# A chain of attention, mixing MLP and gated experts: the expert stage taken apart into steps whose orders are written out in lists

## The chip, the cores and the metric

The kernel runs on one core of a Trainium2 chip. TensorE (PE) multiplies matrices, VectorE (DVE), ScalarE (ACT) and GpSimd (POOL) work on rows, and SyncE (SP) and POOL issue transfers. The metric is the device time of one launch in microseconds (us): the median of several runs.

## The reference

Three layers follow each other on 8 batches of 576 rows of 512 numbers.

```python
attn_out = softmax(q_chunk @ k_chunk.T / 8) @ v_chunk      # 8 heads of 64, chunks of 64 rows
x = sigmoid(xr @ w_r) * (relu(xk @ w_k) ** 2 @ w_v)        # xk, xr: x mixed with the row before
logits = x @ w_gate                                        # 4 experts, the best 2 of a row count
w = softmax over the 2 chosen logits
for e in range(4):                                         # causal attention of width 64
    a = softmax(causal(x @ wq[e] @ (x @ wk[e]).T / 8))
    out += (row chose e) * w * (a @ (x @ wv[e]) @ wo[e])
```

The output has 8 x 576 x 512 numbers in float32. `wq`, `wk` are drawn wide, so that scores are large.

## The kernel before

All matrix products are kept precise by splitting each factor into a high and a low part: `mm3` (L95 to L97) issues hi x hi, lo x hi, hi x lo for each product. Attention weights and V are split too, but with two parts side by side in one operand.

The first 616 us compute the first two layers, in an order written out in the lists `START` and `TWO_UNITS`. They leave the result as `x2T` in DRAM, hi and lo. The function `experts()` does the third layer from 616 us on, and the change lies in it alone.

`experts()` goes through the 8 batches (counted from 0). A batch has two pairs of experts (p) and each pair 9 steps: four query tiles of 128 rows for each of two experts, and the last 64 rows for both experts at once. So a batch has 18 steps (`SB`). A step runs through these functions:

- `t_S`: scores of one tile on PE (L753, `Sps`, as wide as the causal part, 128 to 576 columns), masked negated row maximum on DVE (L755, `sm`, `nm`), Exp on ACT (L765, `P`, with the row sum into `z`).
- `t_T`, three steps later: PE transposes `P` in blocks of 128 (L806, `Tps`), ACT copies the high part (L812, `PTh`), DVE takes the low part (L813, `PTl`).
- `t_AV`, when the tiles of a group (0 to 1, or 2 to 4) are through: PE multiplies with V (L835, L839, `AVps`), ACT copies one half (L849, `yt`), DVE adds the other (L850, `Yf`).
- `t_scale` when a pair is through: the row sums `z` with the gate's weight `gp` on DVE (L778 to L781), transposed on PE (L783), sent through DRAM by SP and spread over the partitions (`zb`). `t_Y`: POOL multiplies `Yf` by `zb` (L855), DVE rounds to `Yh` (L84, also `Y4h` for the last 64 rows), POOL takes the rest `Yl`, `Y4l` (L866).
- `t_out`: output projection (`pj<-woh,Yh`, L95 to L97), ACT copies `o` (L879), SP stores it.

Between the steps lies the preparation of the next pair or batch: `p_load` (POOL issues four loads of `x2`, L616, into the only buffer), `p_qk` (K and Q from `x2`, 12 matmuls of 288 columns for each half; ACT, DVE, copies by SP, and `Ql` on POOL, L649), `p_v` (V and the 4 gate logits in one product of 260 columns; ACT L697, DVE L698, L699), `p_v4` (the last 64 rows of two batches at once, from `x0` loaded at L673) and `p_gate` (L705 to L728: ranks and weights of the experts; seven operations until ACT's Exp L718, five behind it; four of the twelve run on POOL: L709, L711, L717, L723).

Which step issues which piece is fixed by numbers in `CFG`; but the order on each engine is made by the scheduler of the framework, which knows the dependences and a priority for each instruction. Two lines tell it about the filling work:

```python
with tc.issue_after(last.ins) if CFG["after"] else nullcontext():
    for f in fill.get(i, ()):
        f()
```

PSUM gives 2 banks to `Sps`, 3 to `Tps`, 1 to `AVps`, 2 to `pj`; there are 5 buffers of `P` and 3 of `sm`. Each engine takes its instructions strictly in order, so an instruction that waits holds up all behind it on that engine.

Of the kernel before, what the change touches and what calls it, by code (L numbers as in the profile page):

```python
# [59 lines left out]
FIRST_UNITS, FIRST_PAIRS = 2, 6  # L60
CFG = dict(ps=(2, 3, 1, 2), P=5, sm=3, load=5, lag=(3, 4), out=(5, 1), qk1=(1, 1), qk0=(9, 1.1), v=(10, 0.9), order=((3, 0), (2, 0), (0, 0), (4, 0), (1, 0), (3, 1), (2, 1), (0, 1), (1, 1)), after=1, conv='v', clo='v', chi='g', x2hi='g', x2lo='v', ylo='g', yhi='v', xt='aa', r2='av', klo='vv', amul='vv', nearly=2, x2b=1, yb=4, qb=4, direct=((0, 1), (1, 1), (1, 1)), tailAV=4, kp=2, yt=1, yf=2, zb=1, om=(3, 2, 1, 0, 4), hp=1000, x2d=2, early=(2, 1), dact=3, rate0=0.43, rate=0.45, sh=(10, 12, 2), sh2=(11, 1, -1), pro='cccqqaacavvcaaaaacaacaaaascc', alag=2, seq=0, end=2, outL=(11, 2), outE=2, kcp='aa', dsc='v', ldb=2, vb=2, cn=512, stb=2, xb=4, pa=5, tb=2, first_j=7, dve_j=6)
# [514 lines left out]
def experts(tc, at_pool, weights, out, x2T, w_gate, wq, wk, wv, wo, ident, dram, B, S):  # L576
# [3 lines left out]
    nc = tc.nc  # L580
# [11 lines left out]
    groups = [(0, 2), (2, NT)]  # L592

    with ExitStack() as ctx:
# [34 lines left out]
        def p_qk(b, p, nm, h):  # L629
            ws = w_q if nm == "Q" else w_k  # L630
            cc = slice(h * HB, (h + 1) * HB)
            pc = slice(p * 128, (p + 1) * 128)
            pp = ps.tile([128, DM], F32, tag="pj", bufs=CFG["ps"][3], name="pj")[:, :HB]
            x = x2[b]
            mm3(nc, pp, [((ws[g][0][:, pc], ws[g][1][:, pc]), (x.hi[:, g, cc], x.lo[:, g, cc])) for g in range(KD)])
            two = (b * EP + p) % 2
            if nm == "Q":
                if h == 0:
                    for i in range(2):
                        Q[b, 2 * p + i] = px.tile([128, S], F32R, tag="Q", bufs=CFG["qb"], name="Q")  # L640
# [10 lines left out]
            if h == 0:
                K[b, p] = [px.tile([128, S], F32R, tag="Kp" + x, bufs=CFG["kp"], name="Kp" + x) for x in "hl"]
            t, l = K[b, p]
            nc.scalar.activation(out=t[:, cc], in_=pp, func=ACTF.Copy)
            nc.vector.tensor_tensor(l[:, cc], pp, f32(t[:, cc]), op=ALU.subtract)
            if h == 1:
                for i in range(2):
                    KD2[b, 2 * p + i] = d = px.tile([128, SF], F32R, tag="K", bufs=CFG["qb"], name="K")
                    for j in range(2):
                        nc.sync.dma_start(out=f32(d[half[j]]), in_=f32(t[half[i], :SF]))  # L660
                    nc.sync.dma_start(out=f32(KL[two][i][half[i]]), in_=f32(l[half[i], :SF]))
# [6 lines left out]
        def p_v4(b):  # L668

            x = sb.tile([128, 2, KD, 2, 64], F32R, tag="x0", bufs=1, name="x0")  # L670
# [4 lines left out]
            xh, xl = (x[:, i].rearrange("p g j t -> p g (j t)") for i in range(2))  # L675
            pp = ps.tile([128, DM], F32, tag="pj", bufs=CFG["ps"][3], name="pj")[:, :NV]
            mm3(nc, pp, [((xh[:, g], xl[:, g]), (w_v[g][0][:, :NV], w_v[g][1][:, :NV])) for g in range(KD)])
            for j in range(2):
                V4[b + j] = v = V4s[(b + j) % 3]
                G[b + j] = g = sb.tile([128, NT, E], F32, tag="lg", bufs=3, name="lg")  # L680
                r = half[j]
                pv = pp[r, :E * D].rearrange("p (e d) -> p e d", e=E)
                nc.scalar.activation(out=v[:64, :, 0], in_=pv, func=ACTF.Copy)
                nc.vector.tensor_tensor(v[:64, :, 1], pv, f32(v[:64, :, 0]), op=ALU.subtract)
                nc.vector.tensor_copy(g[r, LT], pp[r, E * D:])
                nc.gpsimd.tensor_copy(v[64:, :, 0], f32(v[:64, :, 0]))
# [356 lines left out]
```

## Time and profile before

| | us |
|---|---|
| median of 3 runs | 981.07 (980.85 to 982.61) |
| the profiled run | 981.03 |
| its span, first to last instruction | 978.7 |
| PE busy in the span | 937.5 |
| DVE busy | 662.0 |
| ACT busy | 622.5 |
| POOL busy | 206.0 |
| the expert stage, in the span | 616 to 978.7 |

The profile comes from one execution. A timeline row is one instruction: start, duration, engine, source line, operation, output and inputs with their shapes; in brackets how long the engine stood before it and whose end it waited for. Matmuls overlap, so their rate is read from start to start. A table of stretches gives busy time and the granted clock of PE, 1.00 being full speed.

### The profile page before, as it was taken

What the parts mean: (1) busy time and instruction counts of PE and PEld (TensorE: products, weight loads), DVE (VectorE), ACT (ScalarE), POOL (GpSimd) and SP (SyncE); (2) the same over time, 40 slices, a digit from 0 to 9 for tenths busy, and PEclk for the clock granted to TensorE, in tenths of its full rate; (3) what the DMA queues carried; (4) which work ended last, traced back from release to release, by engine and by line L of the source; (5) the groups of instructions that cost most, each with busy time, mean ns of one, the idle gap of its engine ahead of it and who ended that gap; (6) DMA issues with size and microseconds to landing.
All of it is one profiled execution on the core that took longest, in us unless ns stands there. A gap on an engine that the chain in (4) does not pass through costs nothing.

```text
span 978.7 us, 21549 instructions
## 1 busy us (share of the span) xinstructions
PE 937.5 (96%) x8022; PEld 904.4 (92%) x8022; DVE 662.0 (68%) x1625; ACT 622.5 (64%) x1417; POOL 206.0 (21%) x392
## 2 busy tenths in 40 slices
PE   2689999999999999999999999999999999999997
PEld 2589999999999999999999999898989998999995
DVE  7999746657565755575566612677877787778795
ACT  3598466665756574757576732667675677667684
POOL 3111111101120202020202115513333333323111
PEclk9799999999999999999999999999999999999999
DMA  9884433444324543444322217656362845445322
GB/s 250 203 197 127 87 84 81 86 87 98 83 67 91 114 72 73 81 108 73 77 68 80 59 47 160 135 138 184 68 187 67 211 73 169 123 136 142 99 55 88
DMA packets 223408, 108.39 MB, mean 111 GB/s; under 512 B 187352, under 2 KB 199752, under 8 KB 223304
## 3 DMA queue, kind: packets, MB, share of 16 engines
q1 hardware_dynamic: 193032, 67.16, 30.1%
q0 software_dynamic: 30272, 39.86, 15.5%
q8 instruction: 64, 1.05, 0.5%
q14 instruction: 40, 0.33, 0.1%
HBM read 66.01 MB, written 28.38 MB: 96 GB/s over the span
## 4 chain that ended last, share of the span: by engine, by line
PE 89%; DVE 5%; DMA 4%; issue 1%; ACT 1%; SPq 0%; POOL 0%; POOLq 0%; ACTq 0%; DVEq 0%
PE mps L95 17%; PE mps L96 17%; PE mps L97 17%; PE pj L95 7%; PE pj L96 6%; PE pj L97 6%; PE Sps L753 5%; PE Tps L806 4%; PE AVps L839 2%; PE AVps L835 2%; PE Tps L187 2%; DMA x<-x2T 2%; PE PVps L267 1%; PE Sps L211 1%; DMA ldq<-in_q_dram 1%; DMA st<-in_moe_w_v_dram 1%
## 5 line engine op out<-in xcount | busy, mean ns | idle before, releaser
L95 PE MATMUL mps<-xhk,wkh 128*128 128x384 f32 x384 | 130.7, 340 | 0.0
L95 PE MATMUL mps<-kh,wvh 128*128 128x384 f32 x384 | 129.6, 339 | 0.0
L96 PE MATMUL mps<-xlk,wkh 128*128 128x384 f32 x384 | 129.0, 336 | 0.0
L97 PE MATMUL mps<-xhk,wkl 128*128 128x384 f32 x384 | 129.0, 336 | 0.0
L96 PE MATMUL mps<-kl,wvh 128*128 128x384 f32 x384 | 128.5, 335 | 0.0
L97 PE MATMUL mps<-kh,wvl 128*128 128x384 f32 x384 | 128.4, 334 | 0.0
L370 DVE TENSOR_TENSOR kl<-r,kh 128x384 fp32r<-128x384 f32 x96 | 53.8, 561 | 87.4 <-ACT kh L366 86.8
L765 ACT ACTIVATE P<-sm,nm 128x512 f32<-128x512 f32 (+3 forms) x144 | 83.9, 584 | 22.1 <-DVE nm L755 15.6
L755 DVE CUSTOM_DVE_ANT_0 sm<-Sps,mask 128x256 f32<-128x256 f32 (+4 forms) x160 | 74.5, 477 | 29.5 <-PE Sps L753 28.7
L84 POOL CAST x2d<-x2o 128x384 fp32r<-128x384 f32 x48 | 33.5, 702 | 271.9 <-DVE x2o L387 268.5
L813 DVE TENSOR_TENSOR PTl<-Tps,PTh 128x512 fp32r<-128x512 f32 (+2 forms) x144 | 70.2, 505 | 4.9 <-ACT PTh L812 2.9
L95 PEld LDWEIGHTS mps<-xhk,wkh 128*128 128x128 f32 x384 | 72.2, 188 | 0.6
L95 PEld LDWEIGHTS mps<-kh,wvh 128*128 128x128 f32 x384 | 72.0, 188 | 0.4
L96 PEld LDWEIGHTS mps<-xlk,wkh 128*128 128x128 f32 x384 | 72.2, 188 | 0.0
L97 PEld LDWEIGHTS mps<-xhk,wkl 128*128 128x128 f32 x384 | 72.2, 188 | 0.0
L96 PEld LDWEIGHTS mps<-kl,wvh 128*128 128x128 f32 x384 | 72.1, 188 | 0.0
L97 PEld LDWEIGHTS mps<-kh,wvl 128*128 128x128 f32 x384 | 72.1, 188 | 0.0
L308 DVE SCALAR_TENSOR_TENSOR xa<-XT,mu,xa 128x384 f32<-128x384 f32 x96 | 60.3, 637 | 15.9 <-ACT xa L304 15.7
L364 ACT ACTIVATE r<-mps 128x384 f32<-128x384 f32 x96 | 46.4, 484 | 37.3 <-PE mps L97 37.2
L304 ACT ACTIVATE xa<-XT,mu 128x384 f32<-128x384 f32 x96 | 57.5, 614 | 18.6 <-DVE xlr L319 17.3
L812 ACT ACTIVATE PTh<-Tps 128x512 fp32r<-128x512 f32 (+2 forms) x144 | 61.6, 453 | 8.5 <-PE Tps L806 7.1
L806 PE MATMUL Tps<-ident,P 128*128 128x128 f32 x384 | 63.9, 274 | 2.7 <-DVE z L768 1.4
(183 smaller groups left out, 2629.3 us busy)
## 6 DMA issues: line engine op xcount, KB each, us to landing
x2T<-x2d POOLq DMA_DIRECT2D x48, 384.0 KB, 3.1
x<-x2T POOLq DMA_DIRECT2D x32, 576.0 KB, 6.5
K<-Kph SPq DMA_DIRECT2D x64, 128.0 KB
out_dram<-o SPq DMA_DIRECT2D x32, 256.0 KB
ldk<-in_k_dram SPq DMA_DIRECT2D x192, 32.0 KB
ldq<-in_q_dram SPq DMA_DIRECT2D x192, 32.0 KB
ldv<-in_v_dram SPq DMA_DIRECT2D x21, 256.0 KB
st<-in_moe_w_k_dram SPq DMA_DIRECT2D x8, 512.0 KB
```

Source lines behind the costliest of these rows:

```text
L95: nc.tensor.matmul(out=out, lhsT=ah, rhs=bh, start=first and i == 0, stop=False)
L96: nc.tensor.matmul(out=out, lhsT=ah, rhs=bl, start=False, stop=False)
L97: nc.tensor.matmul(out=out, lhsT=al, rhs=bh, start=False, stop=last and i == n - 1)
L304: nc.scalar.activation(out=a, in_=XT[u][:, g, :, :SEG], func=ACTF.Copy, scale=mu1[:, w, g:g + 1])
L308: nc.vector.scalar_tensor_tensor(a, XT[u][:, g, :, 1:], mu[:, w, g:g + 1], a, op0=ALU.mult, op1=ALU.add)
L370: eng(nc, CFG["klo"][u >= CFG["nearly"]]).tensor_tensor(o.lo, K2.pop((u, m)), f32(o.hi), op=ALU.subtract)
L753: issued = nc.tensor.matmul(out=pp[:, :w], lhsT=x, rhs=y[:, a:a + w], start=n == 0, stop=n == len(terms) - 1)
L755: nc.vector.tensor_tensor_reduce(out=sm[:, a:a + w], in0=pp[:, :w], in1=mk[:, :w], op0=ALU.add, op1=ALU.min, scale=-scale, scalar=3e38, ac ...
L765: nc.scalar.activation(out=x[:, :nk], in_=sm[:, :nk], func=ACTF.Exp, scale=-1.0, bias=nm[:, :1], accum_out=z)
L806: nc.tensor.transpose(pp[:, j], x[:, j * 128:(j + 1) * 128], ident)
L812: nc.scalar.activation(out=h, in_=src, func=ACTF.Copy)
L813: nc.vector.tensor_tensor(l, src, f32(h), op=ALU.subtract)
```

## The change

The functions of the stage are cut at every change of engine. `p_qk` becomes q, qh, ql, kd, qp; `p_v` and `p_v4` become v, vh, vl, vp and lx; `p_gate` gr, ge, gw, gp; `t_S` S, X, E, C; `t_scale` z, zt, zr, zd; `t_T` T, H, L; `t_AV` A, I, F; `t_Y` M, N, O; `t_out` o, oe, od; `p_load` ld. The first 18 steps, batch 0, are scheduled as before. From batch 1 on the pieces are recorded in the order of a list, `TWO_BATCHES` for batches 1 and 2 and again for 3 and 4, `LAST_BATCHES` for 5, 6 and 7, and each instruction is tied to the one recorded before it on its engine, POOL's and SP's transfers included. The four gate operations that ran on POOL run on DVE.

```diff
+FREE_STEPS = 18
+TWO_BATCHES = """
+z-1,1 T-1,15 q0,1,0 S0,2 X0,2 H-1,15 q0,1,1 qh0,1,1 zt-1,1 zr-1,1 L-1,15 E0,2 T-1,17 S0,1 X0,1 S0,0 X0,0 qh0,1,0
...
+""".split()
+LAST_BATCHES = """
+S0,1 T-1,16 z-1,1 X0,1 T-1,17 S0,0 H-1,16 L-1,16 T-1,15 S0,2 X0,0 zt-1,1 X0,2 q0,1,0 E0,1 zr-1,1 zd-1,1 S0,3 H-1,17
...
+""".split()
...
-            nc.gpsimd.tensor_tensor(c1, c1, before.unsqueeze(1).to_broadcast(sh), op=ALU.mult)
+            nc.vector.tensor_tensor(c1, c1, before.unsqueeze(1).to_broadcast(sh), op=ALU.mult)
             nc.vector.tensor_tensor(c2, lj, li, op=ALU.is_gt)
-            nc.gpsimd.tensor_tensor(c1, c1, c2, op=ALU.add)
+            nc.vector.tensor_tensor(c1, c1, c2, op=ALU.add)
...
-            nc.gpsimd.tensor_tensor(x, l, m.unsqueeze(2).to_broadcast([128, NT, E]), op=ALU.subtract)
+            nc.vector.tensor_tensor(x, l, m.unsqueeze(2).to_broadcast([128, NT, E]), op=ALU.subtract)
...
-            nc.gpsimd.tensor_tensor(l, x, m.unsqueeze(2).to_broadcast([128, NT, E]), op=ALU.mult)
+            nc.vector.tensor_tensor(G[b], x, m.unsqueeze(2).to_broadcast([128, NT, E]), op=ALU.mult)
...
-            at(n + L1, lambda b=b, p=p, t=t, i=i: t_T(b, p, t, i))
+            k = divmod(n, SB)
+            at(n + L1, ("T", *k), ("H", *k), ("L", *k))
...
-                last = t_S(*steps[i])
-            with tc.issue_after(last.ins) if CFG["after"] else nullcontext():
-                for f in fill.get(i, ()):
-                    f()
-            for f in todo.get(i, ()):
-                f()
+                first = [("S", *k), ("X", *k), ("E", *k)] + ([("C", *k)] if steps[i][:2] in direct else [])
+            if i >= FREE_STEPS:
+                rest += first + fill.get(i, []) + todo.get(i, [])
+                continue
+            last = run(first[:1]) or last
+            run(first[1:])
+            with tc.issue_after(last.ins):
+                run(fill.get(i, []))
+            run(todo.get(i, []))
...
+        order = [f for b in range(1, B - 3, 2) for f in named(TWO_BATCHES, b)] + list(named(LAST_BATCHES, B - 3))
+        assert sorted(order) == sorted(rest)
+        traced, prior = nc.cur_bb.bb.instructions, {}
+        for f in order:
+            at0 = len(traced)
+            run([f])
+            for ins in traced[at0:]:
+                if ins.engine in prior:
+                    tc.add_manual_dep(ins, prior[ins.engine].name,
+                                      mybir.DependencyInfo(mybir.DependencyClass.NoSync, mybir.DependencyReason.DATA),
+                                      reason="order of the last steps")
+                prior[ins.engine] = ins
```

A name such as `T-1,15` is step 15 of the batch before the list's first. A dependence of class NoSync sets an order and adds no wait of its own.

On POOL, at the load of batch 3's inputs (`x2T_66`; L616 of the kernel before at 717.20 us), the order before is this; `gp` is the gate's weights, `Yf<-Yf,zb` the scaling, `Yl` and `Y4l` the split behind it, `Ql` a copy for the last 64 rows.

```order
L728 COPY gp<-lg 64x2 x2
L616 DMA x_9513<-x2T_66 128x2x576 x4
L855 TENSOR_TENSOR Yf<-Yf,zb 128x576
L649 CAST Ql_7594<-Q 64x64 x4
L866 TENSOR_TENSOR Yl<-Yf,Yh 128x512
L866 TENSOR_TENSOR Y4l<-Yf,Y4h 128x64
L855 TENSOR_TENSOR Yf<-Yf,zb 128x576
L866 TENSOR_TENSOR Yl<-Yf,Yh 128x512
L866 TENSOR_TENSOR Y4l<-Yf,Y4h 128x64
```

The changed kernel has this at the same load (L683 there).

```order
L1013 TENSOR_TENSOR Yf<-Yf,zb 128x576
L1031 TENSOR_TENSOR Yl<-Yf,Yh 128x512
L1031 TENSOR_TENSOR Y4l<-Yf,Y4h 128x64
L1013 TENSOR_TENSOR Yf<-Yf,zb 128x576
L1031 TENSOR_TENSOR Yl<-Yf,Yh 128x512
L1031 TENSOR_TENSOR Y4l<-Yf,Y4h 128x64
L739 CAST Ql_7594<-Q 64x64 x4
L683 DMA x_9625<-x2T_66 128x2x576 x4
L835 COPY gp<-lg 128x2x8
```

The scaling and the split stood behind the load and the copies; now two of each stand ahead of the load, and the gate's weights behind it.

On ACT, where batch 5 begins, the order before is as follows; `V` is the copy of the value projection, `gx` the gate's Exp, `P` the attention's Exp, `Kph` and `Q` copies of projections.

```order
L697 ACTIVATE V_11118<-pj_11266 128x4x64
L849 ACTIVATE yt_11569<-AVps_11564 64x256
L765 ACTIVATE P_11429,z_11430<-sm_11423,nm_11424 128x512
L654 ACTIVATE Kph_11459<-pj_11446 128x288
L765 ACTIVATE P_11444,z_11430<-sm_11438,nm_11439 128x384
L765 ACTIVATE P_11486,z_11430<-sm_11480,nm_11481 128x128
L718 ACTIVATE gx_11314<-gx_11314 128x20
L654 ACTIVATE Kph_11459<-pj_11488 128x288
L812 ACTIVATE PTh2_7973<-Tps_11579 128x4x128
```

The changed kernel has this there; `PTh0` are copies of transposes, and the last V copy is that of `pj_11339`.

```order
L783 ACTIVATE V_11187<-pj_11318 128x4x64
L783 ACTIVATE V_11187<-pj_11339 128x4x64
L998 ACTIVATE yt_11379<-AVps_11372 64x256
L896 ACTIVATE P_11386,z_11044<-sm_11381,nm_11382 128x128
L822 ACTIVATE gx_11400<-gx_11400 128x20
L896 ACTIVATE P_11421,z_11044<-sm_11354,nm_11355 128x256
L965 ACTIVATE PTh0_7971<-Tps_11426 128x128
L896 ACTIVATE P_11470,z_11471<-sm_11431,nm_11432 128x384
L965 ACTIVATE PTh0_7971<-Tps_11434 128x2x128
```

Five instructions stood between the last V copy and the gate's Exp; now two do, and the P of 256 columns (`P_11421`) stands right behind the gate's Exp.

On PE the changed kernel has, from the last matmul of that value projection on:

```order
L159 MATMUL pj_11339<-wv_7341,x2_11050 128x260
L868 MATMUL Sps_11360<-K_10948,Q_10912 128x128
L868 MATMUL Sps_11360<-Kl11_7592,Q_10912 128x128
L990 MATMUL AVps_11372<-PTh0_7971,V_10427 128x256
L986 MATMUL AVps_11372<-PTl0_7972,V_10427 64x128
L986 MATMUL AVps_11372<-PTl0_7972,V_10427 64x256
L990 MATMUL AVps_11372<-PTh0_7971,V_10427 128x256
L868 MATMUL Sps_11423<-K_11402,Q_11283 128x384
L868 MATMUL Sps_11423<-Kl00_7589,Q_11283 128x384
L945 MATMUL Tps_11426<-ident_60,P_11386 128x128
L945 MATMUL Tps_11434<-ident_60,P_11421 128x128 x2
L868 MATMUL Sps_11437<-K_11402,Q_11283 128x512
L868 MATMUL Sps_11437<-Kl00_7589,Q_11283 128x512
```

The transposes of `P_11421` come eight matmuls and one transpose behind the value projection. In the kernel before, an AV group, four score matmuls of 512 and 384 columns and the 12 matmuls of a K projection follow the value projection.

## Rows read from the trace of the kernel before

**Rows 1.** Head of the page and busy time of PE.

```profile
span 978.7 us, 21549 instructions
...
PE 937.5 (96%) x8022; PEld 904.4 (92%) x8022; DVE 662.0 (68%) x1625; ACT 622.5 (64%) x1417; POOL 206.0 (21%) x392
```

**Rows 2.** Stretches: PE, PEld, DVE, ACT, POOL busy (count), granted clock, DMA share, GB/s.

```profile
715.00:728.00 13.00, 12.46 (x86) 11.01 (x85) 12.01 (x42) 11.17 (x34) 6.81 (x11) 1.00 0.78 221
728.00:804.00 76.00, 76.00 (x567) 72.97 (x566) 54.96 (x184) 49.79 (x141) 21.81 (x47) 1.00 0.51 120
804.00:817.00 13.00, 12.45 (x87) 11.05 (x85) 12.01 (x42) 11.16 (x34) 6.80 (x11) 1.00 0.81 225
...
960.00:966.00 6.00, 5.80 (x28) 4.59 (x29) 3.93 (x13) 2.03 (x7) 2.98 (x3) 0.72 0.00 0
```

**Rows 3.** Timeline of PE: start, duration, engine, line, operation, idle before it.

```profile
718.69 0.28 PE L753 MATMUL Sps<-Kl,Q 128*128 128x256 f32 x1
719.08 0.65 PE L839 MATMUL AVps<-PTh,V 128*128 128x320 f32 x3
...
723.44 0.41 PE L806 MATMUL Tps<-ident,P 128*128 128x128 f32 x2 [0.40 <-DVE PTl L813]
723.89 0.50 PE L95 MATMUL pj<-woh,Yh 128*128 128x512 f32 x1
```

**Rows 4.** Timeline of DVE in the same place.

```profile
723.42 0.42 DVE L84 CAST Yh<-Yf 128x512 fp32r<-128x512 f32 x1
```

**Rows 5.** Timeline of POOL in the same place.

```profile
717.20 2.93 POOL L616 DMA_DIRECT2D x<-x2T  x4 [5.62 <-PE pj L97]
720.19 1.42 POOL L855 TENSOR_TENSOR Yf<-Yf,zb 128x576 f32<-128x576 f32 x1
```

**Rows 6.** Timeline of PE: two waits near the end.

```profile
943.27 0.49 PE L753 MATMUL Sps<-K,Q 128*128 128x512 f32 x1 [0.42 <-DVE nm L755]
...
960.13 0.44 PE L806 MATMUL Tps<-ident,P 128*128 128x128 f32 x2 [1.02 <-DVE z L768]
```

**Rows 7.** Timeline of PE: starts without a wait.

```profile
703.56 0.34 PE L753 MATMUL Sps<-K,Q 128*128 128x384 f32 x1
...
703.91 0.28 PE L95 MATMUL pj<-wv,x 128*128 128x260 f32 x1
704.03 0.28 PE L96 MATMUL pj<-wv,x 128*128 128x260 f32 x1
```

**Rows 8.** ACT by line and shape, 640 to 979: busy, mean ns, idle before.

```profile
L765 ACT ACTIVATE P<-sm,nm 128x256 f32<-128x256 f32 x30 | 15.2, 508 | 2.6 <-DVE nm L755 2.1
...
L697 ACT ACTIVATE V<-pj 128x256 fp32r<-128x256 f32 x28 | 10.8, 384 | 13.9 <-PE pj L97 13.8
...
L718 ACT ACTIVATE gx<-gx 128x20 f32<-128x20 f32 x7 | 1.5, 212 | 0.4 <-POOL gx L717 0.3
```

**Rows 9.** DVE by line and shape, 640 to 950, same columns.

```profile
L698 DVE TENSOR_TENSOR V<-pj,V 128x256 fp32r<-128x256 f32 x28 | 11.7, 419 | 3.4 <-ACT V L697 3.0
...
L708 DVE TENSOR_TENSOR c<-lg 128x80 f32<-128x80 f32 x7 | 1.7, 237 | 0.1
```

**Rows 10.** An input load: first issue on POOL, its late reader; below, another load's landing.

```profile
672.25 2.92 POOL L616 DMA_DIRECT2D x<-x2T  x4
...
684.54 0.40 PE L95 MATMUL pj<-x,wk 128*128 128x288 f32 x1 [0.92 <-DMA x<-x2T]
...
x<-x2T POOLq DMA_DIRECT2D x4, 576.0 KB, 5.8
```

**Rows 11.** DVE beside POOL: a slow row, POOL's, and that line's mean.

```profile
667.99 1.07 DVE L759 TENSOR_TENSOR nm<-nm 128x1 f32<-128x1 f32 x1
...
667.63 1.42 POOL L855 TENSOR_TENSOR Yf<-Yf,zb 128x576 f32<-128x576 f32 x1 [1.73 <-issue]
...
L759 DVE TENSOR_TENSOR nm<-nm 128x1 f32<-128x1 f32 x15 | 3.1, 205 | 0.0
```

More of the change, by code (lines that the diff above doesn't have):

```diff
@@ L592, in experts @@
     groups = [(0, 2), (2, NT)]
+    cols = [slice(tiles[a][0], tiles[z - 1][0] + tiles[z - 1][1]) for a, z in groups + [(0, NT)]]
+    SB = EP * len(CFG["order"])
+    steps = [(b, p, t, i) for b in range(B) for p in range(EP) for t, i in CFG["order"]]
+    n = len(CFG["order"])
+    steps[-n:] = [(B - 1, EP - 1, t, i) for g in (1, 0) for t, i in CFG["order"] if groups[g][0] <= t < groups[g][1]]
     with ExitStack() as ctx:
@@ L651, in p_qk @@
[L651 to L661, printed above, removed]
+            mm3(nc, proj((b, p, n), HB), [((ws[g][0][:, pc], ws[g][1][:, pc]), (x.hi[:, g, cc], x.lo[:, g, cc]))
+                                          for g in range(KD)])
@@ new lines, in qk_hi @@
+        def qk_hi(b, p, n):
+            pp, h = PJ[b, p, n], n % 2
+            cc = slice(h * HB, (h + 1) * HB)
+            if n // 2:
+                for i in range(2):
+                    if (b, 2 * p + i) not in Q:
+                        Q[b, 2 * p + i] = px.tile([128, S], F32R, tag="Q", bufs=CFG["qb"], name="Q")
+                for i in range(2):
+                    nc.scalar.activation(out=Q[b, 2 * p + i][half[i], cc], in_=pp[half[i]], func=ACTF.Copy)
+                return
+            if (b, p) not in K:
+                K[b, p] = [px.tile([128, S], F32R, tag="Kp" + x, bufs=CFG["kp"], name="Kp" + x) for x in "hl"]
+            nc.scalar.activation(out=K[b, p][0][:, cc], in_=pp, func=ACTF.Copy)
@@ L664, in experts, with k_copies @@
+        def k_copies(b, p):
+            two, (t, l) = (b * EP + p) % 2, K[b, p]
+            for i in range(2):
+                KD2[b, 2 * p + i] = d = px.tile([128, SF], F32R, tag="K", bufs=CFG["qb"], name="K")
+                for j in range(2):
+                    nc.sync.dma_start(out=f32(d[half[j]]), in_=f32(t[half[i], :SF]))
+                nc.sync.dma_start(out=f32(KL[two][i][half[i]]), in_=f32(l[half[i], :SF]))
         V4s = [sb.tile([128, E, 2, D], F32R, bufs=1, name=f"V4{i}") for i in range(3)]
@@ L702, in p_gate, with v_pool, g_rank @@
+        def v_pool(b):
+            for j in range(2):
+                v, g = V4[b + j], G[b + j]
+                nc.gpsimd.tensor_copy(v[64:, :, 0], f32(v[:64, :, 0]))
+                nc.gpsimd.tensor_copy(g[half[1 - j], LT], g[half[j], LT])
+        def g_rank(b):
             l = G[b]
@@ L911, in experts @@
             nc.gpsimd.memset(before[:, i, 0:i], 1.0)
-        p_gate(0)
+        run([(f, 0) for f in GATE])
         for p in range(EP):
@@ L928, in experts, with at @@
         nc.vector.memset(f32(PTs[0][0][:, :, 1, :128]), 0.0)
[L929 to L934 removed]
         todo, fill = {}, {}
[L937 to L938 removed]
+        def at(i, *fs):
+            todo.setdefault(int(i), []).extend(fs)
         def spread(base, nm, fs):
```

377 lines of the change are left out of this document (249 added, 128 removed).

## The prediction, made before the changed kernel ran

> **What bounds the kernel now.** I read the page's head first, then a table of busy time by stretch, then the matmul timeline at the few stretches that are not full, and there the engine that was waited for. The head gives a span of 978.7 us with PE busy for 937.5 us, 96% [rows 1]; the profiled run took 981.03 us, so 2.3 us lie outside the span, and it stands 0.04 us under the median of 981.07. The sum below is made against the span, and 2.3 us are added at its end. The change touches nothing ahead of the expert stage (from 616 us on). In that stage the long stretches are full: 728 to 804 us shows PE busy for 76.00 of 76.00 us, all at the full clock, while DVE has 54.96 us of work and ACT 49.79 [rows 2]. No order can gain anything there, since the matmuls are the same in both kernels. [...]
>
> **The waits that go.** (1) At 719 to 724 us PE stands three times. Matmuls start 0.12 us apart with 260 columns (703.91 to 704.03) [rows 7] and, as an estimate, half that with 128. Counted from start to start against this, PE is late by 0.27 us at 719.08 (0.39 behind a matmul of 256 columns at 718.69), by about 0.6 at 723.44 (the page's own figure for the idle part is 0.40, since it takes matmuls by their ends), and by 0.23 at 723.89 behind two transposes [rows 3], together 1.1 us. The last of them waits for Yh, the rounding of the attention rows that the output projection reads; DVE has it only at 723.42 [rows 4]. Yh needs the scaled rows from POOL, and POOL does the scaling only at 720.19 because the load of the next batch's inputs stands ahead of it in the queue, issued at 717.20 after POOL had waited 5.62 us for the last matmul that reads the old inputs [rows 5]. The changed order on POOL puts the scaling and the split in front of that load, so the scaling no longer waits for those matmuls. I take all of the 1.1 us: three times, 3.4 us with rounding. From below it is the 0.23 us of the Yh wait alone, 0.7 in all, because the other two pieces wait for DVE and could come back in another order. (2) At 943.27 us PE waits 0.42 us for a row maximum on DVE [rows 6]; with the late starts around it I count 0.7 us, and the new order puts other matmuls between. From below 0. (3) In the tail PE waits 1.02 us for DVE at 960.13 [rows 6], and there are some 4 us more in smaller pieces and at the halved clock. Laying out the new list of the last batch by the same pitches I still find about 3.8 us in waits, against 5.1 now. I take 1.0 us; from above 2.7 if the clock doesn't fall (it ran at half for 3.4 us, worth 1.7), from below -1.7 if it falls twice.
>
> **The waits that come.** (4) Where the second pair of batches ends and the list of the last three begins, the new orders have little matmul work behind the last value projection. PE has two score matmuls of 128 columns, one AV group, the scores of 384 columns and one transpose, and then two transposes of the 256-column P; but on ACT that P's Exp stands behind the gate's Exp, which needs the whole gate, which needs the logits of that last projection. The chain from the last projection matmul's start: 0.28 until its result [rows 7], V's copy 0.384 [rows 8], its difference 0.419, then the logits' copy and seven gate operations, eight small ones at 0.237 each at most [rows 9] and at 0.15 each if their starts overlap (an estimate), 1.2 to 1.9, gate Exp 0.212 and P 0.508 [rows 8]: 3.0 to 3.7 us. PE's work meanwhile: 0.12 for the last projection matmul [rows 7], 0.12 for the two score matmuls of 128 columns, 0.42 for the AV group (three matmuls of 256 columns and one of 128), 0.35 for the scores of 384 columns (703.56 to 703.91) [rows 7] and 0.1 for a transpose, 1.1 us. So PE waits 1.9 to 2.6 us. Behind it the next bank of scores must be freed by the row maximum of the 384 columns, which DVE has behind five gate and three z operations, and this adds 0.1 to 0.6. I take 2.6 us of 2.0 to 3.2, once. Zero would hold only if PE were itself late by so much at that place, which the full stretches speak against. (5) At the beginnings of batches 1 and 3 the transpose of z stands behind 3.4 and 4.3 us of matmul work, and its z on DVE stands behind the whole gate: the same chain to the gate's Exp (about 3.0), and then five gate operations and three of z at 0.2 each (1.6), 4.6 us. That is 1.2 and 0.3 us at most, and nothing where DVE overlaps its starts: 0.5 each, 1.0 in all. (6) The load of x2 has one buffer, so from the last matmul on the old inputs to the first on the new ones PE must live on other work. Before, the orders put 67 to 117 matmuls there, 11.1 to 17.5 us by their pitches; one load is late nevertheless, issued from 672.25 on and waited for at 684.54 for 0.92 us [rows 10], 12.3 us behind the first issue. After, there are 54 to 70 matmuls, 9.5 to 11.9 us. The load issued at 717.20 would need 2.93 us for the four issues [rows 5] and 5.8 us to land [rows 10], 8.7 us, so a load takes 8.7 to 12.3. I take 0.5 us at each of three tight loads, less the one that goes (1.0): +0.4; bounds -1.0 (no load is late) and +4.6 (two of the three tight ones take 12.3: 2 x 2.8 less 1.0).
>
> **What costs nothing.** The four gate operations that move from POOL to DVE add 4 x 0.237 = 0.95 us of DVE per batch [rows 9], in full stretches beside 54.96 of 76.00 us busy [rows 2]; elsewhere than at (4) and (5) the row maxima and differences around them have that room. If not, 7 x 0.95 = 6.6 us. Fewer interruptions of matmul groups change nothing that the pitch rows show. SP's queue gets a fixed order too, with the same K copies and stores; the scale's copies have at least 6.7 us of matmuls before the output projection that needs them.
>
> **The sum.** -3.4 -0.7 -1.0 +2.6 +1.0 +0.4 = -1.1 us: span 977.6, time 979.9 us.
>
> **Rivals.** A, the gains come without the new waits: DVE and ACT catch up in the slack between small instructions, so (4), (5) and (6) fall away and the 684.54 wait goes as well: -3.4 -0.7 -1.0 -1.0 = -6.1, time 974.9 us. For it: DVE and ACT are idle in a quarter to a third of a full stretch [rows 2]. Against it: the order on each engine is binding, so idle time elsewhere doesn't shorten the chain at (4). B, slower: the gate on DVE is held up by POOL. The row minimum at 667.99 took 1.07 us where its line has a mean of 0.205, and it ended as POOL's scaling did (667.63, 1.42 us long) [rows 11]. Before, the gate's multiplications ran on POOL itself, one after the other with the scaling; now seven operations in a row on DVE read two inputs each while POOL may scale (1.42) or split (1.30). With two such hits of 0.87 us at each of the three ends of a list, where the chain has no slack, 5.2 us come on top: -1.1 + 5.2 = +4.1, time 985.1 us. It decides as soon as the gate's chain there is over about 4 us. Against it: the order on POOL has the scaling mostly well before or behind the gate.
>
> [...]
>
> That the list does not do what it says, with the chip running as before, would give 981 us; the bound matmul work makes a result near that likely anyway, and I count it within the forecast.
>
> **How the numbers follow.** About 0.2%, 2 us, is what a measurement here can tell from no change: faster is under 979.1, slower over 983.0. The forecast has 0.45, with its own range of 977 to 983; of it 0.13 lies under 979.1 and 0.30 between, 0.02 over. Rival A has 0.30, nearly all faster (0.28 and 0.02). Rival B has 0.25, of it 0.23 slower and 0.02 between. Together faster 0.41, same 0.34, slower 0.25. The range runs from A's time less 1.4 us (half of the tail's upper bound), 973.5, to just over B's, 985.7.
>
> **What would show it.** Right: in the changed kernel's matmul timeline the output projection behind each input load has no wait for Yh, and POOL shows the scaling ahead of the load; near the start of the sixth batch one wait of 2 to 3 us of the two transposes for ACT's P, with the gate's Exp in front of it. Wrong: that wait is under 1 us (toward A), or row maxima and gate operations take over 0.8 us beside POOL at the ends of lists (toward B); a wait of over 1.5 us for an x2 load would break the term (6); and a tail with more than one stretch at half clock the term (3).

## The result, and the profile after

The changed kernel takes 993.0 us (median of 6 runs, 989.9 to 994.3) against 981.2 us (6 runs, 980.3 to 982.6) for the kernel before: the ratio is 1.0119, with a 95% interval of 1.0107 to 1.0131. It is slower by 11.8 us, where 979.9 us had been forecast, and outside the range. The profiled run took 993.39 us. The page's head, to be read against [rows 1]:

```profile
span 991.6 us, 21443 instructions
...
PE 942.6 (95%) x8022; PEld 907.0 (91%) x8022; DVE 665.4 (67%) x1657; ACT 623.0 (63%) x1417; POOL 195.8 (20%) x360
```

The span is 12.9 us longer with the same 8022 matmuls. Since the matmuls of the expert stage are the same and nearly in the same order of kinds, the two traces can be laid beside each other by matmul work done: at which time has PE got through the same amount? The table is worked out so from all matmul starts, each matmul counted with the usual distance to the next start for its shape; each row is one such amount.

| before, us | after, us | behind, us | what lay in between |
|---|---|---|---|
| 616.2 | 616.5 | 0.3 | |
| 664.5 | 666.0 | 1.5 | batch 0, scheduled in both |
| 688.8 | 691.2 | 2.4 | the first list begins; load of batch 2 |
| 719.6 | 721.7 | 2.1 | |
| 727.5 | 728.9 | 1.4 | the place where PE waited for Yh |
| 736.5 | 742.2 | 5.7 | load of batch 3 |
| 767.8 | 774.9 | 7.1 | the list begins again; load of batch 4 |
| 809.7 | 816.4 | 6.7 | |
| 822.6 | 831.6 | 9.0 | Yh again; load of batch 5 |
| 837.6 | 846.6 | 9.0 | |
| 844.7 | 856.8 | 12.1 | the list of the last three begins |
| 973.8 | 986.9 | 13.1 | batches 5 to 7 and the tail |

So the loss comes in three steps of 4.3, 2.3 and 3.1 us, 9.7 of the 12.8 us between the first row and the last, and some small ones. The 1.4 us between 736.5 and 767.8 us are the largest of these; PE has no wait over 0.25 us there, and they were not traced. The waits of PE from 616 us on, by line and by what was waited for (us in total, times, longest), name the first two:

```profile
PE pj L157 <- DMA x<-x2T: 8.0, 8, 2.5
PE Tps L945 <- ACT P L896: 2.9, 4, 1.5
PE Tps L945 <- DVE P L906: 2.1, 3, 1.4
```

Before, PE waited 1.7 us in all for x2 loads; now 8.0 us. The busy table of stretches (columns as in [rows 2]) shows it around batch 3's load, and below that at the third step:

```profile
724.00:733.00 9.00, 9.00 (x52) 7.78 (x51) 6.05 (x25) 6.00 (x16) 2.85 (x4) 1.00 0.93 279
733.00:736.40 3.40, 0.93 (x8) 0.70 (x6) 0.84 (x4) 0.74 (x3) 0.00 (x0) 1.00 0.77 264
736.40:741.00 4.60, 4.60 (x25) 4.60 (x26) 1.32 (x7) 1.74 (x6) 0.51 (x3) 0.63 0.01 3
...
845.00:853.00 8.00, 5.68 (x42) 4.79 (x42) 7.20 (x33) 3.98 (x15) 2.97 (x9) 1.00 0.29 62
853.00:905.00 52.00, 52.00 (x390) 49.81 (x389) 39.09 (x132) 36.80 (x103) 14.83 (x26) 1.00 0.53 130
```

From 724 to 733 us PE is full. From 733.0 to 736.4 it is busy for 0.93 of 3.40 us while all other engines are nearly idle too and DMA is at 0.77. Then it runs for 4.6 us at a granted clock of 0.63, which means 0.37 x 4.6 = 1.7 us lost on top: from 738 to 740 us the granted clock was 0.50. Behind 853 us PE is full again, at the full clock (52.00 of 52.00, 1.00).

**Why the load is late.** The timeline of POOL there (start, duration, operation, idle before it), to be read against [rows 5]:

```profile
717.55 1.44 POOL L1013 TENSOR_TENSOR Yf<-Yf,zb 128x576 f32<-128x576 f32 x1 [2.49 <-DMA zb<-sc]
...
722.91 0.82 POOL L739 CAST Ql<-Q 64x64 fp32r<-64x64 f32 x3 [0.75 <-DVE Q L730]
723.93 2.92 POOL L683 DMA_DIRECT2D x<-x2T  x4 [0.20 <-PE pj L159]
```

The timeline of PE, to be read against [rows 3], from the last matmul on the old inputs to the late one on the new:

```profile
720.34 0.30 PE L159 MATMUL pj<-x,wq 128*128 128x288 f32 x1
...
722.28 0.48 PE L157 MATMUL pj<-woh,Yh 128*128 128x512 f32 x1
...
732.51 0.30 PE L157 MATMUL pj<-x,wk 128*128 128x288 f32 x1
...
736.35 0.40 PE L157 MATMUL pj<-x,wk 128*128 128x288 f32 x1 [2.47 <-DMA x<-x2T]
```

The timeline of DVE, the first row to be read against [rows 4]:

```profile
719.02 0.43 DVE L146 CAST Yh<-Yf 128x512 fp32r<-128x512 f32 x1 [0.19 <-POOL Yf L1013]
...
722.33 0.94 DVE L730 TENSOR_TENSOR Q<-pj,Q 64x288 fp32r<-64x288 f32 x2 [1.03 <-ACT Q L718]
```

The scaling now stands ahead of the load and runs at 717.55, Yh is ready by 719.45, and the output projection at 722.28 has no wait for it. That part of the change works. But between the scaling and the load stand four Ql copies on POOL, and the last three of them wait for DVE's part of Q, which comes at 722.33 since DVE itself waited 1.03 us for ACT's part. The last matmul that reads the old inputs ended at 720.64; the load is issued at 723.93, 3.3 us later. In the kernel before, it was 0.5 us (716.70 to 717.20 [rows 5]). The load's last quarter then lands at 736.30, 12.4 us after the first issue, where before it took 9.4 us (717.20 to 726.64). The DMA engines in these 12.4 us:

```profile
GB/s 0 0 0 0 37 88 44 81 125 162 258 376 435 383 410 409 413 412 420 398 413 413 420 413 383 394 395 353 363 371 365 387 351 394 364 402 205 34 26 20
...
q0 software_dynamic: 1088, 2.36, 63.9%
q1 hardware_dynamic: 569, 1.04, 23.7%
...
out_dram<-o SPq DMA_DIRECT2D x4, 256.0 KB
```

They move 351 to 435 GB/s for most of the time: 2.36 MB of the load, and 1.04 MB more on the other queue, which are the four output stores that SP issued from 725.03 to 734. In the kernel before, SP issued no store between 717 and 727 us. As an estimate from the row, the stores' 1.04 MB take 2.6 us at some 400 GB/s, of the 3.0 us by which this load took longer.

**The third step** is the wait that the prediction had put at the start of batch 5. The timeline of PE there:

```profile
848.12 0.34 PE L868 MATMUL Sps<-Kl,Q 128*128 128x384 f32 x1
848.97 0.33 PE L945 MATMUL Tps<-ident,P 128*128 128x128 f32 x1 [0.50 <-ACT P L896]
850.77 0.44 PE L945 MATMUL Tps<-ident,P 128*128 128x128 f32 x2 [1.47 <-ACT P L896]
...
852.36 0.33 PE L868 MATMUL Sps<-K,Q 128*128 128x128 f32 x1 [0.35 <-DVE nm L878]
```

The timeline of ACT, the gate's Exp and the P behind it:

```profile
850.00 0.22 ACT L822 ACTIVATE gx<-gx 128x20 f32<-128x20 f32 x1 [1.09 <-DVE gx L817]
850.13 0.49 ACT L896 ACTIVATE P<-sm,nm 128x256 f32<-128x256 f32 x1
```

The timeline of DVE, the row maximum behind the gate and z:

```profile
851.74 0.55 DVE L878 CUSTOM_DVE_ANT_0 sm<-Sps,mask 128x384 f32<-128x384 f32 x1
```

PE waits 0.50 us for one P, 1.47 us for the next, whose Exp starts at 850.13 right behind the gate's Exp at 850.00, and 0.35 us for a bank that the row maximum at 851.74 must free. Counted from start to start the first two are 0.7 and 1.7 us, and the table gives 3.1 us in all.

### The profile page after: what moved, and what is told of

It is laid out like the page before. It is cut to its first block, busy times and chain, and to the rows that moved or that the text cites. A ratio compares the mean times of both kernels' runs of the same rounds, so it can differ in the third digit from the quotient of the medians.

```text
span 991.6 us, 21443 instructions
## 1 busy us (share of the span) xinstructions
PE 942.6 (95%) x8022; PEld 907.0 (91%) x8022; DVE 665.4 (67%) x1657; ACT 623.0 (63%) x1417; POOL 195.8 (20%) x360
## 3 DMA queue, kind: packets, MB, share of 16 engines
q8 instruction: 63, 1.03, 0.4%
## 4 chain that ended last, share of the span: by engine, by line
PE 81%; DMA 8%; DVE 7%; POOL 1%; issue 1%; SPq 1%; ACT 1%; POOLq 0%; DVEq 0%; ACTq 0%
PE mps L157 17%; PE mps L158 17%; PE mps L159 17%; PE pj L157 6%; PE pj L159 5%; PE pj L158 5%; DMA x<-x2T 4%; PE Sps L868 3%; PE Tps L945 3%; PE AVps L990 2%; PE Tps L249 2%; PE AVps L986 2%; PE PVps L329 1%; PE Sps L273 1%; DMA ldq<-in_q_dram 1%
## 5 line engine op out<-in xcount | busy, mean ns | idle before, releaser
L896 ACT ACTIVATE P<-sm,nm 128x384 f32<-128x384 f32 (+4 forms) x144 | 83.5, 581 | 14.0 <-DVE nm L878 11.6
L965 ACT ACTIVATE PTh<-Tps 128x128 fp32r<-128x128 f32 (+4 forms) x160 | 65.2, 434 | 23.9 <-PE Tps L945 22.4
L969 DVE TENSOR_TENSOR PTl<-Tps,PTh 128x512 fp32r<-128x512 f32 (+3 forms) x144 | 71.3, 507 | 7.9 <-ACT PTh L965 6.6
```

Source lines behind the costliest of these rows:

```text
L896: nc.scalar.activation(out=x[:, :sm.shape[1]], in_=sm, func=ACTF.Exp, scale=-1.0, bias=nm, accum_out=z_column(at)[0])
L965: nc.scalar.activation(out=h, in_=src, func=ACTF.Copy)
L969: nc.vector.tensor_tensor(l, src, f32(h), op=ALU.subtract)
```

## The experiments

In all lists the names are those of the change: ld is the load of x2, lx that of the last rows, od an output store, gr to gp the gate, E an Exp, qp the Ql copies, zd the copies of the scale, zt the transpose of z. "PE's stage time" below is from the first score matmul to the last matmul of the profiled run: 357.6 us before, 370.5 us after. Ratios are to the kernel before on the same chip; the changed kernel's is 1.0119 (1.0107 to 1.0131), and gains and losses against it are differences of these ratios. The runs are numbered as their names are; there is no fifth.

**1. The load ahead of the Ql copies** (batches 3 and 5)

```diff
-... qp1,1 S1,12 H1,4 L1,4 A1,0,0 E1,10 T1,10 ld2 I1,0,0 ...
+... N0,1,2 O0,1,2 ld2 qh1,1,2 ... qp1,1 S1,12 H1,4 L1,4 A1,0,0 E1,10 T1,10 I1,0,0 ...
```

> The list of two batches is changed in one place: the load of the second batch's inputs (batches 3 and 5) stands ahead of the four Ql copies on POOL instead of behind them. Theory (the load is issued late: 3.3 us after the last matmul that reads the old inputs, because the Ql copies ahead of it wait for DVE's part of Q): the load is issued about 2.8 us earlier at both places, PE's wait for it falls from 2.5 and 2.7 us to under 0.6 each, and the time falls by 4 to 5.5 us, from 993.0 to about 988. Rival (the load is slow because output stores share the DMA engines, so that it ends when the stores end): it lands no more than 1 us earlier, and the time stays at 991 to 993.

Measured: 987.6 us (986.3 to 989.1), ratio 1.0076 (1.0061 to 1.0091), 0.43% or 4.2 us less than the changed kernel; PE's stage time is 363.0 us. POOL's timeline in this run:

```profile
719.80 2.91 POOL L683 DMA_DIRECT2D x<-x2T  x4
722.70 1.14 POOL L739 CAST Ql<-Q 64x64 fp32r<-64x64 f32 x4
```

PE's timeline, the first matmul on the new inputs:

```profile
731.37 0.30 PE L157 MATMUL pj<-x,wk 128*128 128x288 f32 x1
```

The load is issued at 719.80, 0.3 us behind the last reader, and the Ql copies follow it. The first matmul on the new inputs at 731.37 has no wait and neither have those behind it, though the stores still run beside the load. The late issue was enough to make the wait.

**2. Three stores out of the way of the same loads**

```diff
-... od0,0 ... od0,1 X1,13 od0,3 ... X1,15 od0,2 I1,1,1 zd1,0 H1,12 ...
+... od0,0 ... X1,13 ... X1,15 I1,1,1 zd1,0 od0,1 od0,3 od0,2 H1,12 ...
```

> Three of the four output stores that SP issues while the inputs of batches 3 and 5 are loading are put behind the copies of the next scale; the load itself keeps its place. Theory (late issue only): the load lands within 1 us of where it did, counted from its issue (12.4 us), and the time falls by less than 1.5 us, to 991.5 or more. Rival (sharing with the stores): without about 0.8 MB of stores at some 410 GB/s the load lands about 1.9 us sooner after its issue (10.5 us), both waits of 2.5 to 2.8 us fall by that, and the time falls by about 3.8 us, to 989.

Measured: 988.9 us (985.8 to 993.4), ratio 1.0104 (1.0079 to 1.0129). The four runs lie far apart, and the interval overlaps that of the changed kernel, so the time alone settles nothing. PE's stage time in the profiled run is 363.5 us, 6.9 less, but this run is the fastest of the four: its granted clock over the span is 0.996, that of the slowest 0.985. SP's timeline in this run, the stores:

```profile
722.84 0.36 SPq L1052 DMA_DIRECT2D out_dram<-o  x1
...
742.28 1.51 SPq L1052 DMA_DIRECT2D out_dram<-o  x3
```

PE's timeline, its longest wait for the load of batch 3:

```profile
732.78 0.40 PE L157 MATMUL pj<-x,wk 128*128 128x288 f32 x1 [1.10 <-DMA x<-x2T]
```

With one store beside it in place of four the load of batch 3 lands 11.0 us after its issue (721.74 to 732.74) instead of 12.4, that of batch 5 10.6 instead of 12.7, and the longest wait falls from 2.47 to 1.10 us. The stores are not all of that, since in run 1 the same two loads land 11.2 and 11.1 us after their issue with three of the four stores issued beside them. In run 10, which has both edits, it is 10.3 and 10.8 us. So fewer stores go with a load that is shorter by 0.3 to 2.0 us in all four comparisons, and the sharing counts too, by the traces. My two explanations were not rivals: the load was 3.3 us late and up to 3 us slow, and PE waited for the sum.

**3. The last Exp ahead of the gate's Exp, at the end of the list of two**

```diff
-... gr2 kd2,0 ge2 F1,2,0 gw2 gp2 E1,17
+... gr2 kd2,0 E1,17 ge2 F1,2,0 gw2 gp2
```

> At the end of the list of two batches the last Exp of attention (256 columns) stands ahead of the gate's Exp and the gate's other operations on ACT, instead of behind them. Theory (the two transposes wait for that P, which waits for the gate): PE's wait of 1.47 us before the two transposes at the start of batch 5 goes, and with the waits around it 1.5 to 3 us of the 3.2 us lost there, so 990 to 991.5. Rival (the gate holds DVE anyway, and the scores behind wait for it): the wait moves to the next score matmuls, and less than 0.7 us is gained.

Measured: 994.0 us (993.0 to 995.3), ratio 1.0141 (1.0126 to 1.0156): nothing gained. PE's timeline at the start of batch 5:

```profile
847.67 0.44 PE L945 MATMUL Tps<-ident,P 128*128 128x128 f32 x2 [0.16 <-ACT P L896]
...
850.57 0.33 PE L868 MATMUL Sps<-K,Q 128*128 128x128 f32 x1 [1.66 <-DVE nm L878]
```

The transposes' wait fell to 0.16 us, as the theory said, but the score matmul behind them now waits 1.66 us for DVE's row maximum, as the rival said. Both waits come from the same gate chain on DVE; taking P out of it on ACT moved the wait.

**4. No list at all**

```diff
-FREE_STEPS = 18
+FREE_STEPS = 10000
...
-        order = [f for b in range(1, B - 3, 2) for f in named(TWO_BATCHES, b)] + list(named(LAST_BATCHES, B - 3))
+        order = []
```

> All steps are cut as in the changed kernel and the gate runs on DVE, but no list is used: the framework's scheduler orders all batches as it did batch 0. Theory (the lists' orders cost the 12 us): about 981, 979.5 to 983. Rival (the cut itself, the gate's four operations on DVE, or the load of the last rows issued earlier cost it): 987 to 993.

Measured: 981.9 us (981.1 to 983.6, 10 runs), ratio 1.0014 (1.0003 to 1.0024). PE's waits for the load:

```profile
PE pj L157 <- DMA x<-x2T: 0.4, 1, 0.4
```

Cutting the steps and moving the gate to DVE cost 0.03 to 0.24%, 0.3 to 2.4 us; the lists' orders cost the rest.

**6. The gate later, at batches 3 and 5**

```diff
+        for b, at1, at2 in ((3, ("X", 3, 0), ("L", 2, 17)), (5, ("L", 4, 15), ("X", 5, 3))):
+            gate = [(f, b) for f in GATE]
+            order = [f for f in order if f not in gate]
+            k = order.index(at2) + 1
+            order[k:k] = gate[2:]
+            k = order.index(at1) + 1
+            order[k:k] = gate[:2]
```

> The lists are those of the changed kernel, but at the starts of batches 3 and 5 the twelve gate operations stand behind the first scores' row maxima and Exps of the new batch, on DVE and ACT, instead of ahead of them. Theory (what stands at the boundary is the whole gate chain on DVE, so that moving only ACT's P passed the wait on to the row maxima): both the 1.47 us before the two transposes and the wait for the row maximum go, 2 to 3.2 us less between the first score matmul and the last matmul (370.5 to about 368), time about 990.5. Rival (the V copy and its difference, 0.8 us, hold PE there whatever follows): less than 1 us.

Measured: 996.4 us (994.8 to 997.7), ratio 1.016 (1.0144 to 1.0177), 0.41% or 4.0 us worse than the changed kernel. PE's timeline at batch 3 (first two rows) and at batch 5 (the other two):

```profile
763.41 0.66 PE L945 MATMUL Tps<-ident,P 128*128 128x128 f32 x4 [1.70 <-ACT P L896]
765.29 0.58 PE L990 MATMUL AVps<-PTh,V 128*128 128x256 f32 x1 [1.23 <-DVE Yf L1009]
...
853.29 0.44 PE L945 MATMUL Tps<-ident,P 128*128 128x128 f32 x2 [0.16 <-ACT P L896]
...
858.49 0.33 PE L945 MATMUL Tps<-ident,P 128*128 128x128 f32 x1 [0.81 <-ACT P L896]
```

ACT's timeline at batch 3:

```profile
761.97 0.22 ACT L822 ACTIVATE gx<-gx 128x20 f32<-128x20 f32 x1 [2.60 <-DVE gx L817]
```

At batch 5 the 1.47 us are gone, as wanted, but 0.81 us come back later. At batch 3, where little had been lost, ACT now stands 2.60 us for the gate's Exp with the copies and Exps behind it, and PE waits 1.70 and 1.23 us. The clock adds to this: the stretch from 764.2 to 771.2 us, behind these two waits, was granted 0.51, and that from 979.0 to 986.5 us in the tail 0.54. With 5.91 and 6.40 us of busy time this is about 3 us lost in each, together more than the 4.4 us by which the stage time of this run is longer (374.9 against 370.5). At batch 5 the result is the theory's gain less half, and batch 3 is in neither account: a chain of 3 us in a fixed order has to be put where every engine has other work, and the place that helped at one boundary hurt at the other.

**7. The load of the last rows held back**

```diff
+                if f[0] == "lx" and ins is traced[at0]:
+                    tc.add_manual_dep(ins, prior[pe].name,
+                                      mybir.DependencyInfo(mybir.DependencyClass.Sync, mybir.DependencyReason.DATA),
+                                      reason="load the last rows behind this")
...
-... S0,9 zt0,0 H0,7 X0,11 lx1 oe-1,2 ... I0,0,0 qp0,1 S0,12 ...
+... S0,9 zt0,0 qp0,1 lx1 H0,7 X0,11 oe-1,2 ... I0,0,0 S0,12 ...
```

> In the list of two batches the load of the last rows (x0, right behind the load of x2 for batches 2 and 4 in the changed kernel) is held until the transpose of z has run on PE, as late as in the kernel before; all else as in the changed kernel. Theory (x0's 0.5 MB share the DMA engines with the last quarter of x2): the fourth part of x2 lands 1 to 1.3 us sooner after its issue, PE's two waits of 0.8 us or less shrink to nothing, about 1.5 us in all, 991.5. Rival (stores and the later issue set the landing): under 0.5 us.

Measured: 1002.6 us (1000.7 to 1003.6), ratio 1.0223 (1.0206 to 1.0239). PE's wait at batch 2's load, and at a later place:

```profile
688.22 0.40 PE L157 MATMUL pj<-x,wk 128*128 128x288 f32 x1 [0.31 <-DMA x<-x2T]
...
885.23 0.56 PE L157 MATMUL pj<-wv,x 128*128 128x260 f32 x1 [4.17 <-DMA x<-x2T]
```

The hold acted in the list of the last three as well, and there it made the value projection of batch 6 wait 4.17 us: a fault of the experiment. At batch 2 it did what was meant, the wait fell from 0.80 to 0.31 us; at batch 4 there was no such wait in the changed kernel either. The total says nothing on it.

**8. The edits of runs 1, 2, 6 and 7 together**

> All at once in the lists: the load of batches 3 and 5 ahead of the Ql copies, three of the stores behind the next scale's copies, the gate behind the first row maxima at batches 3 and 5, the load of the last rows held back. Theory (late loads 6 to 7 us, the boundary 3 us, the last rows 1 to 1.5 us make up what the lists lost): 993 - 10.5 = 982.5, 981 to 984.5, level with the kernel before within 0.3%. Rival (the mends pass the waits on, one to the next): 986 or more.

Measured: 995.8 us (995.1 to 996.1), ratio 1.0154 (1.0139 to 1.0169). PE had no wait left at the loads of batches 3 and 5, but the 1.70 and 1.23 us at batch 3 and 4.20 us at batch 6 were there again. Behind the long wait at batch 6 a stretch of 7 us was granted 0.51 here (877 to 884 us) and in run 7 (884.6 to 891.6 us), so that more than the wait itself was lost. The rival held, by the faults of the two edits.

**9. The gate on POOL again**

```diff
-            nc.vector.tensor_tensor(c1, c1, before.unsqueeze(1).to_broadcast(sh), op=ALU.mult)
+            nc.gpsimd.tensor_tensor(c1, c1, before.unsqueeze(1).to_broadcast(sh), op=ALU.mult)
...
```

and so for the other three operations.

> The lists are those of the changed kernel; the four gate operations run on POOL again, as in the kernel before. Theory (where the gate runs is not the cause; its chain is only longer with POOL's four handovers): 993 to 994.5, the wait at the start of batch 5 longer by 0.5 to 1 us. Rival (seven operations in a row on DVE, which POOL's scaling can hold up, cost several us): 990 or less.

Measured: 995.1 us (994.4 to 998.6), ratio 1.0158 (1.0134 to 1.0182). The two transposes at batch 5:

```profile
848.53 0.44 PE L945 MATMUL Tps<-ident,P 128*128 128x128 f32 x2 [1.79 <-ACT P L896]
```

Their wait grew from 1.47 to 1.79 us: the chain is longer with POOL in it, and the gate on DVE was no cost of its own. The run is 0.39% or 3.8 us above the changed kernel, more than the 1.5 us expected. The clock can be all of that: it fell behind three waits here, and behind one in the changed kernel:

```profile
732.00:739.00 7.00, 6.44 (x38) 6.36 (x39) 2.35 (x11) 2.42 (x8) 0.74 (x4) 0.76 0.02 6
825.00:831.00 6.00, 4.66 (x27) 4.47 (x26) 1.06 (x5) 1.64 (x6) 0.74 (x4) 0.72 0.07 27
849.00:855.00 6.00, 5.82 (x33) 5.45 (x32) 3.73 (x17) 3.08 (x10) 0.74 (x4) 0.72 0.03 9
```

The stretch behind the 1.79 us has 0.72, a loss of up to 0.28 x 6 = 1.7 us, and the two others lost about as much each. The two falls more are worth up to 3.4 us, and the stage time of this run is 2.7 us longer (373.1 against 370.5).

**10. The mends, each where its wait was**: the edits of runs 1 and 2; the load of batch 7 ahead of the Ql copies too; the hold of run 7 for batches 2 and 4 alone; the gate later at batch 5 alone and in three places:

```diff
+        for f, at in ((("gr", 5), ("L", 4, 15)), (("ge", 5), ("E", 5, 0)), (("gw", 5), ("L", 5, 0)), (("gp", 5), ("gw", 5))):
+            order.remove(f)
+            order.insert(order.index(at) + 1, f)
```

> The lists with all mends, each where the runs so far showed its wait: the load of batches 3, 5 and 7 ahead of the Ql copies, three stores behind the next scale's copies, the load of the last rows held back for batches 2 and 4 alone, and the gate put later at the start of batch 5 alone, its Exp behind the first three Exps of that batch. Theory (the lists' loss is these waits, and putting the gate later at batch 3 and holding back the last rows of batch 6 made the other waits of the last two runs): from 370.5 us between the first score matmul and the last matmul, 6 to 7 us of load waits with a fall of the clock behind one (1.7), 2 us at batch 5 and 1 us elsewhere go, 360 to 361.5, time 982 to 984. Rival (each mend makes a new wait): 986 or more.

Measured: 982.7 us (980.5 to 987.1, 10 runs), ratio 1.0025 (1.0011 to 1.0039). PE's stage time is 360.2 us. Its waits:

```profile
PE Tps L945 <- DVE P L906: 1.7, 2, 1.3
PE pj L157 <- DMA x<-x2T: 1.6, 3, 0.6
PE Tps L945 <- ACT P L896: 1.6, 4, 0.6
```

Waits for loads fell from 8.0 to 1.6 us, those for ACT's P from 2.9 to 1.6. 0.94 of 1.19% are back, 9.2 of 11.7 us, at the time that the theory gave. That shows late loads and the boundary together, with the clock behind them, to be most of the loss; how much belongs to each edit was measured alone only for the first two, and clearly in time for the first.

**11 and 12. The kernel before with one rule**

```diff
+                if scaled:
+                    tc.add_manual_dep(ld.ins, scaled[-1].name,
+                                      mybir.DependencyInfo(mybir.DependencyClass.NoSync, mybir.DependencyReason.DATA),
+                                      reason="load behind the split")
```

`scaled` holds the scalings on POOL in the first of the two kernels, and the splits into Yl and Y4l in the second.

> The kernel before, scheduled as it is, with one rule more: POOL issues the load of the next inputs behind the last scaling that was recorded ahead of it. Theory (the wait for Yh, 1.1 us three times, comes from the load standing ahead of the scaling, and this load has 9 us to spare there): 0.5 to 1 us less at each of the three places, 978 to 979.5. Rival (the scheduler answers the rule with other orders elsewhere, which cost as much): 980.5 to 983.

> As the run before it, but the load stands behind the last split into Yl and Y4l too. Theory: as there, with Yl 2 us sooner and the load 3 us later: 978 to 979.5. Rival (the load comes too late for the next projections, or other orders cost as much): 981 or more.

Measured: 979.9 us (977.5 to 980.4, 10 runs), ratio 0.9987 (0.9978 to 0.9997), for the first, between its theory and its rival; 978.0 us (975.1 to 979.0, 10 runs), ratio 0.9965 (0.9953 to 0.9977), for the second, which beats both kernels. POOL's timeline in the second, at batch 3's load:

```profile
719.33 1.43 POOL L861 TENSOR_TENSOR Yf<-Yf,zb 128x576 f32<-128x576 f32 x1 [6.20 <-DVE Yf L856]
...
723.75 2.93 POOL L618 DMA_DIRECT2D x<-x2T  x4
```

PE's timeline there, the output projection:

```profile
722.64 0.48 PE L95 MATMUL pj<-woh,Yh 128*128 128x512 f32 x1
```

The scaling comes first, the load is issued only at 723.75, as late as in the changed kernel, and PE doesn't wait for Yh at 722.64. Nor does it wait for this load, since the scheduler left 16.2 us between its old and new readers (718.25 to 734.42), where the changed kernel had 11.9 (720.64 to 732.51). The scheduler changed orders on all engines, so how much of the gain is the Yh wait is not shown.

## Why the prediction was wrong

The step that failed is (6), the x2 loads: "I take 0.5 us at each of three tight loads, less the one that goes (1.0): +0.4". It measured +6.3 us of waits (1.7 to 8.0), and 1.7 us of clock behind the longest of them, past the upper bound of 4.6. Two sentences of the prediction lie behind it. One is on (1): "The changed order on POOL puts the scaling and the split in front of that load, so the scaling no longer waits for those matmuls." It priced what the scaling gains and not what the load loses. The load was counted from its issue, and the issue was taken to follow the last reader at once; but the order on POOL that stood in the same text has the Ql copies ahead of it, and these wait for DVE (run 1). The other is "SP's queue gets a fixed order too, with the same K copies and stores", which counted the stores as costing nothing though their place had moved into the load (run 2). The landing was bounded by 8.7 to 12.3 us, and 12.4 us came at batch 3 and 12.7 at batch 5, so the bound was good to 0.4 us; what was missing was the 3.3 us ahead of the issue. For the same reason the waits did not fall on the loads that the upper bound had in mind, those with the least matmul work between old and new readers. Batches 2, 4 and 6 have 54, 54 and 63 matmuls there and wait 0.8, 0 and 0 us; batches 3, 5 and 7 have 70, 70 and 65, and wait 2.5, 2.5 and 1.1 us, because their loads are issued 3.3, 3.3 and 2.4 us behind the last reader.

(1) The three places are those at 715 and 804 us [rows 2] and, in the trace of the kernel before, 893 to 906 us with PE busy for 12.33 of 13.00 us. The Yh wait went as said: 0.7 us less at batch 3 between the table's rows at 719.6 and 727.5, of the 0.8 (0.6 and 0.23) that had been counted there. At batches 5 and 7 the late load took the gain back in the same stretch. (2) At 943 us nothing was gained: over that amount of work the changed kernel loses 1.5 us where the kernel before lost 1.0. (3) The 1.7 us that the bounds count for the clock are 0.28 of the 6.00 us in [rows 2]; the granted clock there was 0.50 from 962 to 964 us. The tail gave 0.4 us of the 1.0: its clock stayed at the full level (1.00 from 905 to 987 us), but PE waits there too, the longest 1.35 us (see rival B). (4) The boundary at batch 5 was right in place, chain and size: 2.6 us forecast, of 2.0 to 3.2, and 3.1 measured. The split of it was not: the two transposes waited 1.47 us, where 1.9 to 2.6 were forecast, and 0.50 us went to the transpose ahead of them, which waits for an earlier P. (5) The two z transposes cost next to nothing: the one at batch 1 had no wait at 664.55, the one at batch 3 0.15 us at 759.40, where 0.5 each was said. At batch 1 DVE had z by 657.49, ahead of the gate's first operation at 661.91; at batch 3 it had z by 759.25, 3.56 us behind the start of the logits' copy at 755.69. A cost that no step had is batch 0, which was to be as before and lost 1.2 us: its pieces were still scheduled, but from other pieces, and the kernel without lists is 0.3 to 2.4 us slower than the kernel before (run 4), which may be the same. Some 0.4 us of it is a transpose at 619.69 that waits 0.64 us for ACT's P, where the kernel before has 0.23 at 619.00; the rest was not traced.

Rival A fell: the waits of (4) and (6) came, and only those of (5) stayed nearly away. Rival B forecast a slower kernel, but its cause did not occur at the gate. There, in the changed kernel, DVE took 0.234 to 0.245 us in all eight batches at line 809, none near the 1.07 us of [rows 11], and no operation of the gate ran beside a scaling or a split on POOL. Elsewhere the traces do have what B describes. DVE and POOL in the kernel before, at batch 3, and below that in the changed kernel's tail:

```profile
753.99 1.48 DVE L710 TENSOR_TENSOR c<-lg 128x80 f32<-128x80 f32 x1
...
753.93 1.43 POOL L855 TENSOR_TENSOR Yf<-Yf,zb 128x576 f32<-128x576 f32 x1 [1.48 <-DVE Yf L850]
...
976.32 1.09 DVE L906 TENSOR_SCALAR P<-P,z,gp 128x128 f32<-128x128 f32 x1
...
976.07 1.26 POOL L1031 TENSOR_TENSOR Yl<-Yf,Yh 128x512 fp32r<-128x512 f32 x1 [2.43 <-DVE Y4h L146]
```

In the kernel before, one comparison of the gate took 1.48 us here and 1.47 at batch 5, and 0.234 to 0.239 in the six other batches; it ended 0.1 us after POOL's scaling. So an operation in DVE's part of the gate had taken six times its usual length before the change, and the prediction took these hits for something that only the change could bring. In the changed kernel's tail a multiplication of P took 1.09 us beside POOL's split, and 0.35 at three other places with the same shape; PE's wait of 1.35 us is for this one. In both pairs POOL's operation had started first, by 0.06 and 0.25 us; that it made DVE's slow is not shown, since no run was made to tell the two apart.

## What to carry to other kernels

When a load has one buffer, count from the last reader of the old contents to the landing of the new, in four parts: what stands ahead of the load in its queue and what that waits for, the issues, the bytes of every other transfer in that window, and only then the matmul work that has to cover it. A written order binds in both directions: whatever is put ahead of something delays it by all that the new neighbour waits for (the load behind the Ql copies was issued at 723.93, ahead of them in run 1 at 719.80). And the chain through three engines that gates the order boundary here was not mended on one of them (run 3); look first for who waits on the other two.

## What the runs showed that I had not expected

A wait of PE for 2.47 us was followed by 4.6 us at a granted clock of 0.63 (table of stretches above), so it cost 4.2 us and not 2.5. The same load's wait of 2.36 us in run 6 and of 2.31 us in run 7 was followed by a granted clock of 0.50 from 737 to 740 and from 738 to 741 us. Shorter waits differ from run to run: the 1.47 us wait at 850.77 had no such cost, but in run 1 the stretch at the same place (842 to 847.5 us) was granted 0.69. And a rule of a few lines for the scheduler gained 0.35%, where the kernel with two lists of together some thousand entries, which fixed every order from batch 1 on, lost 1.19%.
